# Attention into two gated layers on one core: the first tile's products in plain float32, its weights split only for the later tiles, conversion by whole blocks, and another order at layer two's border

## The chip, the cores and the metric

The kernel runs on one core of a Trainium2 chip. The metric is the device time in microseconds (us) of one execution; of several executions the median counts. The engines are TensorE (PE in the profile, with its weight loads as PEld), VectorE (DVE), ScalarE (ACT), GpSimd (POOL) and SyncE (SP), which here only issues DMAs.

## The reference

```python
# attention: q, k, v are [4, 8, 576, 64]; causal softmax plus a memory term
scores = np.where(causal, -1e9, q @ k.T / 8);  a = softmax(scores);  local = a @ v
mem_out = (phi(q) @ M_prev) / (phi(q) @ z_prev + 1e-6)     # phi(x) = elu(x) + 1
out = g * mem_out + (1 - g) * local                        # g = sigmoid(beta), one per head
x = out as [2304 tokens, 512]
# layer one and layer two: w_in [512, 2048], w_out [2048, 512] each
h = x @ w_in;  x = (h * sigmoid(1.702 * h)) @ w_out
h = x @ w_in;  x = (h * clip(h + 3, 0, 6) / 6) @ w_out
```

The weights arrive as float64, seen by the kernel as pairs of 32-bit words, and are made float32 on the chip.

## The kernel before

**Tiles.** The 2304 tokens are six tiles of 384. Tiles 0, 1, 3 and 4 hold the first 384 rows of a batch entry; tiles 2 and 5 hold the last 192 rows of two entries each. Attention runs by pairs of heads, four pairs to a segment (`scores`, `turn`, `mem_read`, `weigh`), and is emitted some pairs ahead of the layers: while tile t goes through layer one, attention makes the x of tile t + 1. `pump` sets the pace: `PG0` and `PG1` say over what share of a tile's 128 quarter-steps the attention steps are spread.

**Layers.** `moe` goes through units (layer, tile, f), f over 16 blocks of 128 hidden columns. A unit is four products into the bank h (`kk` 0 to 3, L302 to L304), a gate chain, and, `lag` units later, four products into the banks y0 to y3 (`emit_y`, L282 to L284). Each product is three matmuls on float32r operands that were split in two parts: w hi by x hi, w lo by x hi, w hi by x lo. In the first five tiles of layer one h has one bank and the lag is 1; from the last tile of layer one on h has three banks and the lag is 3.

**The gate.** ACT makes tanh (L254) or relu (L258) of h, DVE multiplies with h (L256, L260), ACT rounds to g hi (L263), and POOL, in tile 0 DVE, subtracts to get g lo (L265). x is split in the same way by `split_x` (ACT L247, DVE L248).

**Weight conversion.** `conv_w` takes a half block (w_in part a = 0 or w_out part a = 1 of one f; 128x512 pairs of words) through a chain in six stages: two DVE operations on the words (L197, L202); POOL adds a constant (L206) and ACT or DVE takes the absolute value (L208, L210); ACT takes the sign (L212); DVE makes the float32 value x in a temporary tile (L215); ACT rounds it to the hi part (L222); POOL (layer one) or DVE (layer two) subtracts for the lo part (L225). A chain is emitted stage by stage through `Chains.step`, once for every product; at most four halves are under way, since `conv_w` first finishes the half four before. The first operation is pinned in DVE's program order for layer one (`PIN`), free for layer two. The halves of layer one are converted during the attention of tile 0 and during tile 0's products; those of layer two from the last tile of layer one on, one every seven steps (`PR`).

**Order on the engines.** The instructions are put in each engine's queue by a planner with its own costs, within what `issue_after`, `after_gates` and `keep_in_program_order` fix.

**The border of the layers.** x of layer two's tile 0 is split after each of the last h products of layer one (`after_quarter`); layer two's first h products are emitted while three units of layer one's y are still pending.

Of the kernel before, what the change touches and what calls it, by code (L numbers as in the profile page):

```python
# [22 lines left out]
NT = 384  # L23
PRE = 4
KQ = 80
CR = 3.75
OFF = 3
PG0 = 0.55
# [25 lines left out]
AHEAD = 4  # L54
TF = 12
TWB = (1, 3)
EARLY = 3
P2 = 4
PR = 7
# [45 lines left out]
def attention_moe_kernel(ctx: ExitStack, tc: tile.TileContext, qk0, sk0, sk1, vm0, vm1, bb, w1, w2, out):  # L105
# [15 lines left out]

    wt = {}
    w_raw = {}
    w_gen = {}
    w_jobs = [(layer, f, a) for layer in range(2) for f in range(NF) for a in range(2)]
    w_at = [0, 0]
    w_temp = {}
# [22 lines left out]
    def load_w(n):  # L150


        while w_at[0] < min(n, len(w_jobs)):
            key = layer, f, a = w_jobs[w_at[0]]
            w_at[0] += 1
            if (layer, f, a) == (0, NF - 1, 0):
                for old in range(2 * TF, 2 * (TF + 1)):
                    gen = w_gen.get(w_jobs[old - 2])
                    if gen is not None:
                        chains.finish(gen)  # L160
                w_temp.clear()
            pool, tag = slot(*key)
            w_raw[key] = pool.tile([128, 2 * DM], I32, tag=tag, bufs=1, name=f"r{f}{a}")
            move(0, out=w_raw[key], in_=(w1, w2)[layer][f, a].bitcast(I32))

    def slot(layer, f, a):

        if layer == 1 and f < EARLY:
            return early[0], f"e{f}{a}"
        return wp, f"w{f - EARLY * layer}{a}"  # L170

    def temp(layer, f, a):

        if layer == 0 and f < TF:
            k = (2 * f + a) % 4
            if k // 2 not in w_temp:
                w_temp[k // 2] = wp.tile([128, 2, DM], F32, tag=f"w{NF - 1}{k // 2}", name="wtemp")
            return w_temp[k // 2][:, k % 2]
        pool, bufs = temps
        return pool.tile([128, DM], F32, tag="wt", bufs=bufs, name="wt")  # L180

    def conv_w():

        n = w_at[1]
        key = layer, f, a = w_jobs[n]
        if n >= 4 and w_jobs[n - 4] in w_gen:
            chains.finish(w_gen[w_jobs[n - 4]])
        w_at[1] += 1
        load_w(w_at[1])
        if layer == 0:  # L190
            load_w(min(2 * NF, w_at[1] + AHEAD))
        z = 2 if layer == 1 else int(2 * f + a >= 2 * PRE)
        words = w_raw.pop(key).rearrange("p (n two) -> p n two", two=2)
        lo, hi = words[:, :, 0], words[:, :, 1]

        def chain():
            first = DVE.tensor_scalar(  # L197
                out=lo, in0=lo, scalar1=29, scalar2=0x40000000, op0=ALU.logical_shift_right, op1=ALU.bitwise_or
            )
# [14 lines left out]
            x = temp(layer, f, a)  # L214
            DVE.scalar_tensor_tensor(  # L215
                out=x, in0=f32(lo), scalar=BIG, in1=f32(hi), op0=ALU.min, op1=ALU.mult
            )
            pool, tag = slot(layer, f, a)
            t = pool.tile([128, 2, DM], F32R, tag=tag, bufs=1, name=f"w{f}{a}")
            wt[key] = t  # L220
            yield
            ACT.copy(out=t[:, 0], in_=x)  # L222
            yield
            e = "DVE" if (2 * f + a) % WLE[z][1] < WLE[z][0] else "POOL"
            {"DVE": DVE, "POOL": POOL}[e].tensor_tensor(out=t[:, 1], in0=x, in1=f32(t[:, 0]), op=ALU.subtract)  # L225

        w_gen[key] = chains.start(after_gates(chain(), CB[layer]))

# [22 lines left out]
    def gate(layer, ti, h, g):  # L251
        t = gp.tile([128, NT], F32, tag="t", bufs=GB, name="t")
        if layer == 0:
            ACT.activation(out=t, in_=h, func=AF.Tanh, scale=0.851)  # L254
            yield
            d = DVE.scalar_tensor_tensor(out=t, in0=t, scalar=1.0, in1=h, op0=ALU.add, op1=ALU.mult)  # L256
# [8 lines left out]
        d = (DVE, POOL)[GLE[ti if layer == 0 else -1]].tensor_tensor(out=g[:, 1], in0=t, in1=f32(g[:, 0]), op=ALU.subtract)  # L265
        gated[("DVE", "POOL")[GLE[ti if layer == 0 else -1]]].append(d.ins)

    def moe(units, before_h, after_quarter, finish):
# [4 lines left out]
        def emit_y():  # L273
            layer, ti, f, g, gen = pend.pop(0)
            chains.finish(gen)
            w = need_w(layer, f, 1)
            if f == 0:
                for d in range(KD):
                    ys[d] = psy.tile([128, NT], F32, tag=f"y{d}", name=f"y{d}")
            for d in range(KD):  # L280
                o = d * 128
                PE.matmul(ys[d], lhsT=w[:, 0, o:o + 128], rhs=g[:, 0], start=(f == 0), stop=False)  # L282
                PE.matmul(ys[d], lhsT=w[:, 1, o:o + 128], rhs=g[:, 0], start=False, stop=False)  # L283
                PE.matmul(ys[d], lhsT=w[:, 0, o:o + 128], rhs=g[:, 1], start=False, stop=(f == NF - 1))  # L284
                if f == NF - 1:
                    finish(layer, ti, d, ys[d])
                chains.step()
                if d == KD - 1 and layer == 0 and ti == LAST:
                    load_w(2 * (NF + EARLY + f + 1))
                yield layer, ti, f  # L290

        ys = [None] * KD
        for layer, ti, f in units:
            before_h(layer, ti, f)
            w = need_w(layer, f, 0)
            h = phase["h"].tile([128, NT], F32, tag=phase["tag"], bufs=phase["bufs"], name="h")
# [12 lines left out]
            g = phase["g"].tile([128, 2, NT], F32R, tag="g", bufs=phase["lag"] + 1, name="g")  # L309
            gen = chains.start(gate(layer, ti, h, g))  # L310
# [87 lines left out]
    def attention(ap):  # L398
# [253 lines left out]
        def weigh(i):  # L652
# [28 lines left out]
            if ((0, ti), p) not in xr:  # L681
                xr[(0, ti), p] = xp.tile([128, NT], F32, tag=f"x{p}", name=f"x{p}")
# [55 lines left out]
    with ExitStack():  # L738
# [19 lines left out]
        POOL.memset(step_down, -STEP)  # L758

# [50 lines left out]
        stream = moe(units, before_h, after_quarter, finish)  # L810

        with tc.tile_pool(name="ap", bufs=2) as ap:
# [3 lines left out]
            for k, mark in enumerate(att):  # L816
# [3 lines left out]
                convert_to(min(2 * PRE, int(2 * PRE * k / KQ) + K0))  # L820
            convert_to(2 * PRE)
            banks[0] = 3
            phase["behind"] = lambda: marks[-1 - SLACK] if len(marks) > SLACK else None
            for kk in range(KD):
                split_x((0, 0), kk)
            qi, ti = 0, 0
            for layer, t, f in stream:
# [7 lines left out]
                if ti == 0:  # L835
                    convert_to(min(2 * NF, 2 * PRE + int(qi / CR)))
                pump((qi - OFF) / (PG0 * 128 / 36 if TILES[ti + 1][0][1] == 0 else PG1 * 128 / 57))

        with tc.tile_pool(name="x2p", bufs=2) as x2p:
# [4 lines left out]
            load_w(2 * (NF + EARLY))  # L844
# [64 lines left out]
```

## Time and profile before

| | before |
|---|---|
| median of 3 runs | 1082.98 us (1082.46 to 1084.0) |
| the profiled execution | 1084.36 us, span 1082.5 us |
| mean granted clock | 0.980 |
| PE busy | 1033.4 us, 95% of the span |
| DVE, ACT, POOL busy | 510.2, 498.8, 399.1 us |
| DMA | 71.91 MB, 19.7% of the span of 16 engines |

The busy shares are means over stages with different limits, so they are read by stages: tile 0 of layer one (50 to 188 us), a middle tile, the border of the layers (602 to 737 us), and layer two after it. The duration of a matmul in a row is its time from start to modelled end; matmuls overlap, so what one costs is the distance between starts.

### The profile page before, as it was taken

Reading aid. Unit: us, or ns where it says so; the run is one execution under the profiler, and the core shown is the slowest. Engines: PE = TensorE matmul, PEld = TensorE weight load, DVE = VectorE, ACT = ScalarE, POOL = GpSimd, SP = SyncE. Lnnn points to the kernel's source line nnn. Section 1 sums busy time; section 2 is a strip of 40 time slices with the busy share of each in tenths; the row PEclk is TensorE's granted clock in tenths of the full one; section 3 lists DMA queues with packets and bytes.
Section 4 is the critical chain, followed back from the end, with each engine's and each line's share of the span. In section 5 each row is a group of like instructions: output and inputs, shape, how many; then the busy total and the mean of one; then the engine's idle time right before and its main releaser. Section 6 shows DMA issues by size and latency. Waiting matters only on the chain. (4 is left out here: it accounts for less than half of the span.)

```text
span 1082.5 us, 16719 instructions
## 1 busy us (share of the span) xinstructions
PE 1033.4 (95%) x6153; PEld 940.3 (87%) x6153; DVE 510.2 (47%) x1372; ACT 498.8 (46%) x1152; POOL 399.1 (37%) x444
## 2 busy tenths in 40 slices
PE   7877888999999999999999997998999999999998
PEld 4566766888888888888889997998999999999998
DVE  6999997344544443333444598873121121211210
ACT  6757655334454454433333566764233232332322
POOL 4778765223333333222322454543222222222221
PEclk9888998999999999999999998999999999999999
DMA  6643321211121110211110684001010010100000
GB/s 227 239 158 103 127 69 36 68 45 59 28 76 37 38 55 25 59 30 60 30 30 16 246 324 140 30 1 59 1 31 30 1 59 1 31 30 1 30 1 29
DMA packets 29280, 71.91 MB, mean 66 GB/s; under 512 B 3600, under 2 KB 12816, under 8 KB 29200
## 3 DMA queue, kind: packets, MB, share of 16 engines
q1 hardware_dynamic: 29200, 70.86, 19.7%
q8 instruction: 48, 0.79, 0.3%
q14 instruction: 32, 0.26, 0.1%
HBM read 61.41 MB, written 9.44 MB: 65 GB/s over the span
## 5 line engine op out<-in xcount | busy, mean ns | idle before, releaser
L265 POOL TENSOR_TENSOR g<-t,g 128x384 fp32r<-128x384 f32 x176 | 185.1, 1052 | 473.1 <-ACT g L263 448.5
L302 PE MATMUL h<-xs,w 128*128 128x384 f32 x768 | 267.1, 348 | 16.1 <-DVE t L256 8.1
L282 PE MATMUL y<-g,w 128*128 128x384 f32 x768 | 260.4, 340 | 3.4 <-ACT g L263 3.3
L303 PE MATMUL h<-xs,w 128*128 128x384 f32 x768 | 260.1, 339 | 0.3 <-DVE w L225 0.3
L304 PE MATMUL h<-xs,w 128*128 128x384 f32 x768 | 260.3, 339 | 0.0
L283 PE MATMUL y<-g,w 128*128 128x384 f32 x768 | 259.2, 337 | 0.0
L284 PE MATMUL y<-g,w 128*128 128x384 f32 x768 | 244.1, 339 | 0.6 <-POOL g L265 0.6
L260 DVE SCALAR_TENSOR_TENSOR t<-t,h 128x384 f32<-128x384 f32 x96 | 53.1, 553 | 273.2 <-ACT t L258 273.2
L302 PEld LDWEIGHTS h<-xs,w 128*128 128x128 f32 x768 | 146.3, 191 | 24.7 <-DVE t L256 12.6
L282 PEld LDWEIGHTS y<-g,w 128*128 128x128 f32 x768 | 145.1, 189 | 7.0 <-ACT g L263 4.6
L284 PEld LDWEIGHTS y<-g,w 128*128 128x128 f32 x768 | 142.3, 188 | 6.7 <-issue 4.1
L303 PEld LDWEIGHTS h<-xs,w 128*128 128x128 f32 x768 | 146.6, 191 | 1.4 <-issue 0.8
L304 PEld LDWEIGHTS h<-xs,w 128*128 128x128 f32 x768 | 146.0, 190 | 1.1 <-issue 0.5
L283 PEld LDWEIGHTS y<-g,w 128*128 128x128 f32 x768 | 145.1, 189 | 1.4 <-issue 1.3
L263 ACT CAST g<-t 128x384 fp32r<-128x384 f32 x192 | 98.4, 513 | 95.1 <-DVE t L260 49.2
L258 ACT ACTIVATE t<-h,three 128x384 f32<-128x384 f32 x96 | 55.7, 580 | 170.5 <-PE h L304 170.5
L454 POOL TENSOR_SCALAR p<-p,st,omg 128x128 f32<-128x128 f32 (+3 forms) x128 | 91.8, 729 | 99.3 <-DVE st L450 44.7
L446 ACT ACTIVATE p<-s,st 128x256 f32<-128x256 f32 (+4 forms) x160 | 82.4, 521 | 69.6 <-DVE st L441 57.5
L441 DVE CUSTOM_DVE_ANT_0 s<-s,mask 128x128 f32<-128x128 f32 (+3 forms) x144 | 72.6, 526 | 85.0 <-PE s L381 84.1
L256 DVE SCALAR_TENSOR_TENSOR t<-t,h 128x384 f32<-128x384 f32 x96 | 52.7, 550 | 74.5 <-ACT t L254 70.3
L381 PE MATMUL s<-qk 64*128 64x256 f32 (+5 forms) x384 | 72.3, 466 | 12.2 <-issue 3.5
L254 ACT ACTIVATE t<-h 128x384 f32<-128x384 f32 x96 | 46.7, 490 | 67.9 <-PE h L304 65.1
(79 smaller groups left out, 1103.5 us busy)
## 6 DMA issues: line engine op xcount, KB each, us to landing
r<-in_w_dram SPq DMA_DIRECT2D x64, 512.0 KB, 6.2
vm<-in_vm_dram SPq DMA_DIRECT2D x16, 386.0 KB, 3.0
qk<-in_qk_dram SPq DMA_DIRECT2D x16, 384.0 KB, 3.5
qk<-in_sk_dram SPq DMA_DIRECT2D x32, 192.0 KB, 3.3
x2d<-yo SPq DMA_DIRECT2D x24, 192.0 KB, 1.9
xr<-x2d SPq DMA_DIRECT2D x24, 192.0 KB, 3.1
out_dram<-yo SPq DMA_DIRECT2D x24, 192.0 KB, 1.9
vm<-in_vm_dram SPq DMA_DIRECT2D x16, 258.0 KB, 2.7
```

What stands on the lines that cost most here:

```text
L263: gated["ACT"].append(ACT.copy(out=g[:, 0], in_=t).ins)
L265: d = (DVE, POOL)[GLE[ti if layer == 0 else -1]].tensor_tensor(out=g[:, 1], in0=t, in1=f32(g[:, 0]), op=ALU.subtract)
L282: PE.matmul(ys[d], lhsT=w[:, 0, o:o + 128], rhs=g[:, 0], start=(f == 0), stop=False)
L283: PE.matmul(ys[d], lhsT=w[:, 1, o:o + 128], rhs=g[:, 0], start=False, stop=False)
L284: PE.matmul(ys[d], lhsT=w[:, 0, o:o + 128], rhs=g[:, 1], start=False, stop=(f == NF - 1))
L302: PE.matmul(h, lhsT=w[:, 0, c:c + 128], rhs=x[:, 0], start=(kk == 0), stop=False)
L303: PE.matmul(h, lhsT=w[:, 1, c:c + 128], rhs=x[:, 0], start=False, stop=False)
L304: PE.matmul(h, lhsT=w[:, 0, c:c + 128], rhs=x[:, 1], start=False, stop=(kk == KD - 1))
L381: ins = PE.matmul(out, **args).ins
L441: DVE.tensor_tensor_reduce(out=o, in0=o, in1=m, scale=-SCALE, scalar=init, op0=ALU.add, op1=ALU.min, accum_out=out)
L446: return ACT.activation(out=dst, in_=o, func=AF.Exp, scale=-1.0, bias=m, accum_out=s)
L454: (DVE, POOL)[e[norms[0] % len(e)]].tensor_scalar(out=dst, in0=dst, scalar1=s, scalar2=w, op0=ALU.mult, op1=ALU.mult)
```

## The change

It keeps what is computed and changes these parts.

1. Tile 0 of layer one uses plain float32 operands: one matmul call per product on the unsplit weight, x and g. There the split of x, the rounding of g and the subtraction for g lo are left out (`exact`).
2. `conv_w` takes a whole block f (both parts a, 128x1024) at a time. For layer one the chain ends with the float32 value, written in the raw block's own place (`wx[f]`). One block before must be fully emitted. For layer two the constant is added on ACT instead of POOL, and the split is part of the chain.
3. Layer one's weights are split for tiles 1 to 5 by `part_w`: from step 104 of tile 0 on, one block every 8 steps, two DMAs copy the block's value to temporary tiles, then two ACT roundings and two DVE subtractions write the parts where the block was.
4. At the border `between` splits x for layer two, then all pending y of layer one is emitted, then layer two's first h.
5. The last three units of layer one subtract for g lo on DVE (`GLL`); paces are restated: `CR`, `PG0` (0.85 in tile 0, 0.55 as before otherwise), `PR` 14 for whole blocks, `AHEAD`, `W0`, `TWB`.

```diff
-CR = 3.75
+CR = 7.5
-PG0 = 0.55
+PG0 = (0.85, 0.55)
+GLL = 3
-W0 = (2, 3)
-WLE = ((0, 2), (0, 2), (2, 2))
-ABS = ((0, 2), (1, 2), (2, 2))
+W0 = (1, 2)
+ABS = ((0, 1), (1, 2), (1, 1))
-AHEAD = 4
-TF = 12
-TWB = (1, 3)
+AHEAD = 2
+TWB = (3, 2)
+S2 = 104
+SR = 8
-PR = 7
+PR = 14
...
     def conv_w():
-        n = w_at[1]
-        key = layer, f, a = w_jobs[n]
-        if n >= 4 and w_jobs[n - 4] in w_gen:
-            chains.finish(w_gen[w_jobs[n - 4]])
+        key = layer, f = w_jobs[w_at[1]]
+        if (layer, f - 1) in w_gen:
+            chains.finish(w_gen[layer, f - 1])
...
+        words = raw.rearrange("p a (n two) -> p a n two", two=2)
+        lo, hi = words[:, :, :, 0], words[:, :, :, 1]
+        if layer == 0:
+            wx[f] = f32(raw)[:, :, 0:DM]
...
-            POOL.tensor_scalar(out=f32(hi), in0=f32(hi), scalar1=STEP, scalar2=1.0, op0=ALU.add, op1=ALU.mult)
+            if layer == 0:
+                POOL.tensor_scalar(out=f32(hi), in0=f32(hi), scalar1=STEP, scalar2=1.0, op0=ALU.add, op1=ALU.mult)
+            else:
+                ACT.activation(out=f32(hi), in_=f32(hi), func=AF.Identity, bias=step_up[:, 0:1])
...
+            x = [wx[f]] if layer == 0 else [temp() for _ in range(2)]
+            for k, to in enumerate(x):
+                at = slice(None) if layer == 0 else k
+                DVE.scalar_tensor_tensor(
+                    out=to, in0=f32(lo)[:, at], scalar=BIG, in1=f32(hi)[:, at], op0=ALU.min, op1=ALU.mult
+                )
+            if layer == 1:
+                yield
+                yield from parts(layer, f, x)
...
+    def parts(layer, f, x):
+        pool, tag = slot(layer, f)
+        t = pool.tile([128, 2, 2, DM], F32R, tag=tag, bufs=1, name=f"w{f}")
+        wt[layer, f] = t
+        for a in range(2):
+            ACT.copy(out=t[:, 0, a], in_=x[a])
+        yield
+        for a in range(2):
+            DVE.tensor_tensor(out=t[:, 1, a], in0=x[a], in1=f32(t[:, 0, a]), op=ALU.subtract)
+
+    def part_w(f):
+        def chain():
+            x = [temp() for _ in range(2)]
+            for a in range(2):
+                move(4, out=x[a], in_=wx[f][:, a])
+            del wx[f]
+            yield
+            yield from parts(0, f, x)
+        if (0, f - 1) in w_gen:
+            chains.finish(w_gen[0, f - 1])
+        w_gen[0, f] = chains.start(after_gates(chain(), CB[1]))
...
+        exact = (layer, ti) == (0, 0)
+        to = g[:, 0] if exact else t
...
+        if exact:
+            return
...
+                if (layer, ti) == (0, 0):
+                    PE.matmul(ys[d], lhsT=w[:, o:o + 128], rhs=g[:, 0], start=(f == 0), stop=(f == NF - 1))
...
+            if (layer, ti, f) == (1, 0, 0):
+                between()
+                while pend:
+                    yield from emit_y()
...
+                    if exact:
+                        PE.matmul(h, lhsT=w[:, c:c + 128], rhs=x, start=first, stop=last)
...
-            if layer == 0 and f == NF - 1:
-                split_x((0, ti + 1) if ti < LAST else (1, 0), kk)
+            if layer == 0 and f == NF - 1 and ti < LAST:
+                split_x((0, ti + 1), kk)
...
+        def between():
+            for kk in range(KD):
+                split_x((1, 0), kk)
...
-            for kk in range(KD):
-                split_x((0, 0), kk)
...
-                    convert_to(min(2 * NF, 2 * PRE + int(qi / CR)))
+                    convert_to(min(NF, PRE + int(qi / CR)))
+                if ti < 2 and 128 * ti + qi >= S2:
+                    part_to(1 + (128 * ti + qi - S2) // SR)
```

## Rows read from the trace of the kernel before

**Rows 1.** Busy time of each engine, granted clock and DMA share in four stages.
```profile
50.00:188.00 138.00, 115.54 (x636) 94.42 (x635) 128.57 (x288) 86.52 (x192) 97.41 (x87) 0.90 0.32 108
188.00:278.00 90.00, 89.64 (x582) 78.44 (x581) 37.42 (x145) 36.38 (x99) 26.86 (x33) 1.00 0.18 53
602.00:737.00 135.00, 127.11 (x709) 123.75 (x707) 111.43 (x162) 93.35 (x169) 66.30 (x62) 0.97 0.40 145
800.00:1082.00 282.00, 279.14 (x1611) 278.82 (x1609) 44.73 (x82) 88.83 (x168) 66.79 (x66) 1.00 0.07 23
```
**Rows 2.** DVE's groups by line in 50 to 188 us: busy, mean ns, idle before.
```profile
L202 DVE SCALAR_TENSOR_TENSOR r<-r 128x512 int32<-128x512 int32 x29 | 26.1, 909 | 0.1
L197 DVE TENSOR_SCALAR r<-r 128x512 int32<-128x512 int32 x29 | 19.8, 684 | 0.1
L215 DVE SCALAR_TENSOR_TENSOR wtemp<-r 128x512 f32<-128x512 f32 x21 | 18.3, 871 | 0.8 <-ACT r L212 0.8
...
L265 DVE TENSOR_TENSOR g<-t,g 128x384 fp32r<-128x384 f32 x16 | 11.6, 728 | 0.0
```
**Rows 3.** Single lines over the whole span: shortest, median and longest duration in ns.
```profile
L197 DVE TENSOR_SCALAR r<-r x64: 410/421/1517, 22.0 to 730.8; 128x512 int32<-128x512 int32 x64
L202 DVE SCALAR_TENSOR_TENSOR r<-r x64: 673/747/1778, 22.4 to 731.8; 128x512 int32<-128x512 int32 x64
L215 DVE SCALAR_TENSOR_TENSOR wtemp<-r x24: 667/681/1770, 25.8 to 145.4; 128x512 f32<-128x512 f32 x24
```
**Rows 4.** POOL's groups by line in 50 to 188 us.
```profile
L225 POOL TENSOR_TENSOR w<-wtemp,w 128x512 fp32r<-128x512 f32 x22 | 32.3, 1474 | 9.8 <-ACT w L222 9.8
L206 POOL TENSOR_SCALAR r<-r 128x512 f32<-128x512 f32 x29 | 25.0, 867 | 13.1 <-DVE r L202 10.5 <-DMA qk<-in_sk_dram 1.2 <-DVE st L449 0.7
L225 POOL TENSOR_TENSOR w<-wt,w 128x512 fp32r<-128x512 f32 x8 | 10.9, 1364 | 6.9 <-ACT w L222 6.9
```
**Rows 5.** Timeline of PE in layer two, 24 matmuls apart: start and duration in us.
```profile
800.26 0.33 PE L282 MATMUL y<-g,w 128*128 128x384 f32 x1
...
804.42 0.33 PE L282 MATMUL y<-g,w 128*128 128x384 f32 x1
```
**Rows 6.** Timeline of PE at plain float32 matmuls of the attention.
```profile
24.50 0.83 PE L366 MATMUL mem<-vm,phi 128*128 128x130 f32 x6
25.18 0.49 PE L396 MATMUL t<-ident,p 128*128 128x128 f32 x3
```
**Rows 7.** One DVE operation at two widths, groups by shape over the span.
```profile
L441 DVE CUSTOM_DVE_ANT_0 s<-s,mask 128x512 f32<-128x512 f32 x48 | 32.9, 704 | 51.1 <-PE s L381 51.1
...
L441 DVE CUSTOM_DVE_ANT_0 s<-s,mask 128x128 f32<-128x128 f32 x32 | 9.7, 308 | 7.2 <-PE s L381 7.2
```
**Rows 8.** Busy times in the two disturbed stretches of the border.
```profile
650.00:670.00 20.00, 14.15 (x65) 12.41 (x64) 17.02 (x26) 14.32 (x27) 8.74 (x8) 0.83 0.37 127
730.00:750.00 20.00, 17.03 (x86) 15.82 (x85) 9.69 (x16) 9.99 (x20) 6.92 (x7) 0.91 0.13 40
```
**Rows 9.** PE's longest wait in 600 to 760 us: total, times, longest in us.
```profile
PE h L302 <- ACT xs L247: 5.1, 2, 3.7
```
**Rows 10.** Conversion groups of ACT and DVE in 602 to 737 us.
```profile
L212 ACT ACTIVATE r<-r,step_down 128x512 f32<-128x512 f32 x32 | 24.2, 768 | 6.2 <-POOL r L206 6.0
L208 ACT ACTIVATE r<-r 128x512 f32<-128x512 f32 x32 | 21.7, 681 | 23.2 <-DVE r L202 23.1
L222 ACT CAST w<-wt 128x512 fp32r<-128x512 f32 x32 | 19.6, 619 | 7.9 <-DVE wt L215 7.6
L263 ACT CAST g<-t 128x384 fp32r<-128x384 f32 x30 | 15.3, 510 | 1.6 <-DVE t L256 1.3 <-DVE t L260 0.2
...
L202 DVE SCALAR_TENSOR_TENSOR r<-r 128x512 int32<-128x512 int32 x32 | 38.2, 1209 | 0.1
L225 DVE TENSOR_TENSOR w<-wt,w 128x512 fp32r<-128x512 f32 x32 | 25.3, 798 | 2.7 <-ACT w L222 2.7
```
**Rows 11.** DMA issues over the span: count, KB each, median us to landing.
```profile
xr<-x2d SPq DMA_DIRECT2D x24, 192.0 KB, 3.1
```

More of the change, by code (lines that the diff above doesn't have):

```diff
@@ L124, in attention_moe_kernel @@
     w_gen = {}
-    w_jobs = [(layer, f, a) for layer in range(2) for f in range(NF) for a in range(2)]
+    w_jobs = [(layer, f) for layer in range(2) for f in range(NF)]
     w_at = [0, 0]
-    w_temp = {}
+    w_parted = [0]
     temps = []
@@ L153, in load_w, with slot @@
         while w_at[0] < min(n, len(w_jobs)):
[L154 removed]
+            key = layer, f = w_jobs[w_at[0]]
             w_at[0] += 1
[L156 to L166, printed above, removed]
[L168 to L180 removed]
+            pool, tag = slot(layer, f)
+            w_raw[key] = pool.tile([128, 2, 2 * DM], I32, tag=tag, bufs=1, name=f"r{f}")
+            for a in range(2):
+                move(0, out=w_raw[key][:, a], in_=(w1, w2)[layer][f, a].bitcast(I32))
+    def slot(layer, f):
+        if layer == 1 and f < EARLY:
+            return early[0], f"e{f}"
+        return wp, f"w{f - EARLY * layer}"
     def conv_w():
[L184 to L187 removed]
+        key = layer, f = w_jobs[w_at[1]]
+        if (layer, f - 1) in w_gen:
+            chains.finish(w_gen[layer, f - 1])
         w_at[1] += 1
@@ L213, in chain, with temp @@
             yield
[L214 to L220, printed above, removed]
-            yield
[L222 to L227, printed above, removed]
+            x = [wx[f]] if layer == 0 else [temp() for _ in range(2)]
[7 more added lines that the diff above has]
+                yield from parts(layer, f, x)
+        w_gen[key] = chains.start(after_gates(chain(), CB[layer]))
+    def temp():
+        pool, bufs = temps
+        return pool.tile([128, DM], F32, tag="wt", bufs=bufs, name="wt")
+    def parts(layer, f, x):
+        pool, tag = slot(layer, f)
+        t = pool.tile([128, 2, 2, DM], F32R, tag=tag, bufs=1, name=f"w{f}")
[8 more added lines that the diff above has]
+            x = [temp() for _ in range(2)]
+            for a in range(2):
+                move(4, out=x[a], in_=wx[f][:, a])
+            del wx[f]
+            yield
+            yield from parts(0, f, x)
+        if (0, f - 1) in w_gen:
+            chains.finish(w_gen[0, f - 1])
+        w_gen[0, f] = chains.start(after_gates(chain(), CB[1]))
     def convert_to(n):
@@ L231, in convert_to, with part_to, need_w @@
             conv_w()
-    def need_w(layer, f, a):
-        convert_to(2 * (NF * layer + f) + a + 1)
-        gen = w_gen.pop((layer, f, a), None)
+    def part_to(n):
+        while w_parted[0] < min(n, NF):
+            w_parted[0] += 1
+            part_w(w_parted[0] - 1)
+    def need_w(layer, ti, f, a):
+        convert_to(NF * layer + f + 1)
+        if (layer, ti) != (0, 0) and layer == 0:
+            part_to(f + 1)
+        gen = w_gen.pop((layer, f), None)
         if gen is not None:
             chains.finish(gen)
-        return wt[layer, f, a]
+        return wx[f][:, a] if (layer, ti) == (0, 0) else wt[layer, f][:, :, a]
     xr = {}
@@ L255, in gate @@
             yield
-            d = DVE.scalar_tensor_tensor(out=t, in0=t, scalar=1.0, in1=h, op0=ALU.add, op1=ALU.mult)
+            d = DVE.scalar_tensor_tensor(out=to, in0=t, scalar=1.0, in1=h, op0=ALU.add, op1=ALU.mult)
         else:
@@ L264, in gate, with moe @@
         yield
-        d = (DVE, POOL)[GLE[ti if layer == 0 else -1]].tensor_tensor(out=g[:, 1], in0=t, in1=f32(g[:, 0]), op=ALU.subtract)
-        gated[("DVE", "POOL")[GLE[ti if layer == 0 else -1]]].append(d.ins)
-    def moe(units, before_h, after_quarter, finish):
+        e = "POOL" if GLE[ti if layer == 0 else -1] and not (layer == 0 and ti == LAST and f >= NF - GLL) else "DVE"
+        d = {"DVE": DVE, "POOL": POOL}[e].tensor_tensor(out=g[:, 1], in0=t, in1=f32(g[:, 0]), op=ALU.subtract)
+        gated[e].append(d.ins)
+    def moe(units, before_h, after_quarter, between, finish):
         pend = []
@@ L275, in emit_y @@
             chains.finish(gen)
-            w = need_w(layer, f, 1)
+            w = need_w(layer, ti, f, 1)
             if f == 0:
@@ L308, in moe @@
                     yield layer, ti, f
-            g = phase["g"].tile([128, 2, NT], F32R, tag="g", bufs=phase["lag"] + 1, name="g")
-            gen = chains.start(gate(layer, ti, h, g))
+            g = phase["g"].tile([128, 2, NT], F32 if exact else F32R, tag="g", bufs=phase["lag"] + 1, name="g")
+            gen = chains.start(gate(layer, ti, f, h, g))
             chains.step()
@@ L758, in attention_moe_kernel @@
         POOL.memset(step_down, -STEP)
+        step_up = const.tile([128, 1], F32, name="step_up")
+        POOL.memset(step_up, STEP)
         gall = const.tile([128, 4, H], F32, name="gall")
```

50 lines of the change are left out of this document (29 added, 21 removed).

## The prediction

> **What bounds the kernel now.** I read the busy times by stages first. From 800 us on PE is full, at full clock: 279 of 282 us, and a matmul of a split product starts every 0.173 us (24 of them in 4.16 us) [rows 1, 5]. A middle tile is the same, 89.6 of 90 us. Whatever leaves such a stretch on another engine is worth nothing there. Two stretches are different. In tile 0 of layer one (50 to 188 us) DVE is busy 128.6 of 138 us, and PE's granted clock is 0.90 on average [rows 1]. So tile 0 is set by DVE. There the reader is to look at DVE's groups: the three large ones of the weight conversion (L202, L197, L215) take 909, 684 and 871 ns on average where their shortest take 673, 410 and 667 [rows 2, 3]. The longest take over 1500. Meanwhile POOL is busy 97.4 us of the 138 [rows 1], 43.2 of them with the weights' lo parts [rows 4]. These three read and write SBUF alone, and seem to be held while POOL works. The other weak stretch is the border of the layers, 602 to 737 us: PE is busy 127.1 of 135. In 650 to 670 us it starts 65 matmuls where 20 / 0.173 = 115 fit, a loss of 50 x 0.173 = 8.7 us; in 730 to 750 us 86, a loss of 5.1 [rows 8]. The longest wait there is for the split of x, 3.7 us [rows 9].
>
> **Tile 0: what goes from DVE.** The conversion has 29 halves left in the window. The three groups come to 26.1 + 19.8 + 29 x 0.871 = 71.2 us (eight of the L215 write another tile; I charge them the same mean) [rows 2]. At the shortest durations they would be 29 x (0.673 + 0.410 + 0.667) = 50.8; so 20.4 us are stretch.
> - Whole blocks: one DVE operation at 128 and 512 columns takes 308 and 704 ns, so 176 ns do not depend on width [rows 7]. Three operations less per block, 14.5 blocks: 7.7 us saved. The abs operations, fewer too, I leave at nothing.
> - The weights' lo parts leave POOL: 43.2 us of 97.4 [rows 4, 1]. If stretch follows POOL's busy time, 44% of 20.4 goes: 9.0 us. Bounds: nothing (if the stretch is the remaining POOL work's) and 20.4. I take 9.0, since both kinds of POOL work are of similar length.
> - g lo leaves DVE: 11.6 us [rows 2].
> - Split of the first blocks comes back from step 104 on: three blocks, two subtractions each at 0.798 (the same operation at the border [rows 10]): 4.8 us.
>
> DVE's new load is 128.6 - 7.7 - 9.0 - 11.6 + 4.8 = 105.1 us. That is all for a tile that took 138.
>
> **Tile 0: what PE gets.** Here the change costs. Before, a product is three matmuls, 3 x 0.173 = 0.520 us. No row shows a plain float32 product of 384 columns with 128x128 weights. The nearest are the attention's plain matmuls of 130 columns: a pair of a first segment makes three such calls and has six matmuls in the trace, so a call is two; six take 25.18 - 24.50 = 0.68 us, 0.113 each [rows 6]. Scaled to 384 columns a matmul is 0.335, a product 0.669. From below: two matmuls no faster than split ones, 0.347. From above: the scaled value, as a fixed part would only lower it. I take 0.669, because the row is plain float32 too. So 128 products cost 85.6 us instead of 66.6: 19.0 more. The remaining 636 - 384 = 252 matmuls of the window are attention's; at 0.113 they are 28.5 us [rows 1, 6] (that window may hold a few products of the tile before or after). PE's load becomes 114.1 us and passes DVE's 105.1. PE becomes the bound.
>
> The Trainium skill speaks against the change at this place: the page "FP8 and Floating Point Precision", section "TensorE Precision Notes", says that true FP32 takes four passes through the array. With a split product as three single passes that would be 4/3 of 0.520, or 0.693 a product, 3.1 us more for the tile than my scaled row. No row of this trace has the product itself.
>
> How well is a bound filled? DVE filled 128.6 of 138, 0.93 [rows 1]. With two engines nearly level I take the same: 114.1 / 0.93 = 122.7 us. **Tile 0 falls from 138 to 122.7, 15.3 us less.** Bounds: 114 (PE as full as in a middle tile) to 138.
>
> ACT loses in the same window the rounding of weights and of g; it was busy 86.5 of 138, so nothing follows. The split of x ahead of tile 0 is hidden behind attention's last matmuls and I cost its removal at nothing; if that cover were gone it would be about 1 us (a rounding of 0.51 as L263 and a subtraction like L265).
>
> **Tile 1: what comes back.** Thirteen blocks are split here. DVE gets 26 subtractions at 0.798, 20.7 us, on its 37.4 of 90; ACT gets 26 roundings at 0.619, 16.1 us, on 36.4 [rows 1, 10]. Both stay under 60 of 90, so PE keeps the bound. But h has one bank: the next h waits for tanh and multiply (about 0.51, as L263, and 0.57, by rows 7: 0.176 + 384 x 0.00103), hidden behind the y products of 4 x 0.520 = 2.08. An operation just begun delays these by at most 0.62 on ACT and 0.80 on DVE; 1.08 + 1.42 = 2.50, beyond the cover by 0.42. Over thirteen units that is at most 5.5 us, and a second operation in a row would add. Below it is nothing. I take 3.
>
> The copies are 32 DMAs of 256 KB on SP's queue. A 192 KB transfer lands in 3.1 us [rows 11], 256 KB then in about 4.1, and DMA is busy 0.18 of the tile [rows 1]. Each waits for a temporary tile (three, and a block takes two), that is, for the subtractions of the block before; behind it in SP's queue stand attention's loads, and the stores of tile 0's y, whose three buffers the gate shares. Loads are prefetched two pairs ahead. A late store would hold the gate on ACT; the copies begin 24 steps, about 20 us, before their block is used. So I take nothing, and up to 4 us above.
>
> **The border.** Splitting x ahead of the pending y gives it three y blocks of cover, 3 x 2.08 = 6.2 us, where the trace shows a wait of 3.7 and then cold PE. That cover is longer than the wait. Of the 8.7 us lost in 650 to 670 I take 6.0 as recovered; the gate waits before the split stay. Bounds 0 and 8.7. The loss of 5.1 in 730 to 750 I leave as it is; it can go, or grow (below). POOL loses the 32 constant additions (about 0.9 each) and ACT gets them at about 0.68, as L208 [rows 10]: 21.8 us on 93.4 of 135 [rows 1], so ACT reaches 115, or 0.85. It still fits.
>
> **Sum** against the profiled execution's 1084.4 us: 1084.4 - 15.3 + 3 - 6 = 1066.1. That execution is 1.4 above the median of the runs; on the median's scale 1064.7, stated as 1064.
>
> **Rivals.**
> *The conversion chain in series.* One block must be emitted before the next starts, and layer one's first operation is pinned behind it on DVE, where four halves could overlap before. At the window's means a block is DVE 1.19 + 1.64, POOL 1.73, ACT 1.54 (L212), DVE 1.57: 7.7 us; at DVE's shortest 6.2. With tile 0 at 122.7, block 15 is wanted 115 us after its start; with two blocks ready by then, 14 remain, 8.2 us each. From there on it decides. If queues add 1.5 to 7.7, 14 x 9.2 = 129, plus the last unit's 7, is 136: tile 0 gains 2 and the time is 1064.7 + 13.3 = 1078. For: DVE is a full queue. Against: it becomes emptier by 23 us, POOL by 43.
>
> *The border's conversion too slow: the other side.* Layer two's block, in whole pieces, is DVE 2 x 0.42 (L197's median) + 2 x 1.21, ACT three passes 2 x (0.68 + 0.68 + 0.77), then 2 x 0.68 on DVE (L215's median), 2 x 0.62 on ACT, 2 x 0.80 on DVE [rows 3, 10]: 11.7 us in a row, 10.7 with two fixed parts of 0.18 saved and the first rounding beside the second L215. Before, 32 halves took the stretch of 135 us, 8.4 a block, with four halves under way. If blocks go one by one at 10.7, the last is ready 16 x 2.3 = 37 us later, and layer two's tile 0 waits: 1065 + 37 = 1102. It decides from 8.4 + 18.3 / 16 = 9.5 us a block on. For it: two temporary tiles, just one block's. Against it: the first operations aren't pinned there, so the next block can start on DVE while ACT works; ACT's own work is 2 x 2.75 a block at most, and 2 x 0.51 per 4.16 us for gates, 7.3 us a block at the limit.
>
> *PE not relieved at all.* If tile 0's clock falls as before (0.90), a plain product costs up to twice as much in those stretches, 114.1 / 0.90 = 126.8 before any wait, and with 0.93 136. Then the conversion gain is spent on PE: 1064.7 + 13 = 1078, the first rival's time.
>
> **From this to the numbers.** A measurement of this kernel tells about 0.2%, 2.2 us. Forecast (1050 to 1073): 0.55. First and third rival (1073 to 1080.8): 0.20. No change: 0.06. Slower, by the border: 0.14. Better than 1050, with tile 0 at PE's load and both border losses gone (1084.4 - 24 - 13.8 = 1047): 0.05. Faster is 0.80. The range 1046 to 1082 takes in the bounds and all but the slow side; the forecast's own is 1050 to 1073.
>
> **What would show it.** Right: tile 0 ends near 173 us, its plain matmuls start 0.33 us apart, DVE's L202 means less per column and POOL is busy near 54 us there; tile 1 stays 90 to 93; PE's wait for the split of x at the border is gone. Wrong: in tile 0 PE waits for L215's successor (first rival), a clock below 0.9 (third), or PE waits at the border for ACT's rounding or DVE's subtraction, with the last conversion later than 737 (second).

## The result, and the profile after

| | before | after |
|---|---|---|
| median | 1082.72 us (1082.27 to 1084.0) | 1063.97 us (1063.95 to 1064.1) |
| ratio, 95% interval | | 0.9825 [0.9808, 0.9842] |
| span, mean clock | 1082.5 us, 0.980 | 1062.2 us, 0.990 |
| PE, DVE, ACT, POOL busy | 1033.4, 510.2, 498.8, 399.1 us | 1035.6, 486.7, 495.0, 317.9 us |

The kernel is 1.75% faster, 18.8 us. To see where, I cut every trace at the same marks: PE's first matmul for h, and ACT's first reading of y (yo) of each tile. The lengths in us, with those of the experiments (each experiment's ratio below is against the kernel before on its own chip):

| run | median | first h | tile 0 | tile 1 | tiles 2 to 4 | border (tile 5 and layer two's tile 0) |
|---|---|---|---|---|---|---|
| before | 1082.7 | 50.2 | 142.1 | 108.2 | 306.7 | 143.9 |
| after | 1064.0 | 45.9 | 123.5 | 117.3 | 307.3 | 136.8 |
| e1_border_undone | 1057.4 | 46.1 | 123.5 | 117.3 | 307.3 | 130.2 |
| e2_border_only | 1084.3 | 50.4 | 140.6 | 108.1 | 306.7 | 145.3 |
| e3_pace_055 | 1068.3 | 46.9 | 130.1 | 114.6 | 307.0 | 136.2 |
| e8_own_yo | 1060.0 | 48.9 | 122.6 | 117.2 | 307.4 | 130.8 |
| e4_no_lo | 1056.4 | 47.9 | 111.2 | 114.1 | 306.7 | 142.9 |
| e5_one_matmul | 1077.2 | 49.0 | 138.1 | 106.7 | 306.7 | 142.9 |
| e7_no_lo_parts | 1065.3 | 45.6 | 125.1 | 117.5 | 306.9 | 136.2 |
| e6_pool_add | 1068.9 | 47.0 | 123.7 | 117.3 | 307.4 | 139.9 |
| e9_lo_on_dve | 1074.0 | 47.7 | 130.3 | 112.5 | 306.7 | 143.1 |
| e10_act_add | 1071.8 | 50.8 | 140.6 | 108.3 | 306.7 | 132.1 |
| e11_all_act | 1053.5 | 48.1 | 118.3 | 117.3 | 307.0 | 130.6 |
| e12_pool_out | 1054.1 | 47.0 | 126.6 | 107.4 | 306.7 | 131.7 |

Layer two after its tile 0 takes 331.4 to 331.8 us in all of them. So the change starts tile 0 4.3 us earlier, takes 18.6 us from tile 0, gives 9.1 back in tile 1, and takes 7.1 at the border.

The busy times of the changed kernel by stages (stretch, length, PE, PEld, DVE, ACT, POOL, granted clock, DMA), to be read beside [rows 1]:
```profile
46.00:166.00 120.00, 112.44 (x461) 64.87 (x463) 95.94 (x200) 59.20 (x117) 48.80 (x40) 0.99 0.41 144
166.00:276.00 110.00, 108.27 (x705) 91.48 (x702) 70.63 (x222) 59.19 (x154) 33.35 (x43) 1.00 0.35 114
592.00:727.00 135.00, 129.50 (x730) 128.86 (x729) 103.44 (x141) 106.59 (x161) 39.64 (x30) 0.97 0.39 140
```
In tile 0 the fuller engine is no longer DVE (128.6 of 138) but PE (112.4 of 120), and the clock goes from 0.90 to 0.99. Cut at 90 us, the tile has two parts:
```profile
46.00:90.00 44.00, 36.94 (x153) 21.00 (x154) 40.96 (x83) 23.67 (x48) 27.67 (x21) 0.96 0.75 266
90.00:166.00 76.00, 75.50 (x310) 43.87 (x310) 54.98 (x118) 35.52 (x70) 21.13 (x20) 1.00 0.21 73
```
In the first DVE is still the full engine (41.0 of 44, PE 36.9); in the second it is PE (75.5 of 76). DVE's and POOL's conversion groups there, whole blocks now, answer to [rows 2, 4] (the changed kernel has other line numbers: DVE's L187, L192 and L210 are L197, L202 and L215 of the kernel before, POOL's L197 is its L206, ACT's L205 its L212):
```profile
L192 DVE SCALAR_TENSOR_TENSOR r<-r 128x1024 int32<-128x1024 int32 x15 | 21.5, 1433 | 0.2
L210 DVE SCALAR_TENSOR_TENSOR r<-r 128x1024 f32<-128x1024 f32 x15 | 18.6, 1240 | 8.8 <-ACT r L205 8.8
L187 DVE TENSOR_SCALAR r<-r 128x1024 int32<-128x1024 int32 x15 | 11.4, 757 | 0.0
```
```profile
L197 POOL TENSOR_SCALAR r<-r 128x1024 f32<-128x1024 f32 x15 | 19.1, 1276 | 31.3 <-DVE r L192 21.3 <-DVE st L496 8.8 <-DMA r<-in_w_dram 1.2
```
A block costs DVE 1.433 + 1.240 + 0.757 = 3.43 us against 2 x (0.909 + 0.684 + 0.871) = 4.93 before. The plain products on PE's timeline, to set beside [rows 5, 6]:
```profile
91.78 2.74 PE L317 MATMUL y<-g,r 128*128 128x384 f32 x8
94.36 0.49 PE L443 MATMUL t<-ident,p 128*128 128x128 f32 x3
```
Eight matmuls take 94.36 - 91.78 = 2.58 us, 0.3225 each. A plain call shows as two matmuls in the trace, so a plain product is 0.645 us against 0.520 split. At the border the split of x no longer holds PE, but something else does (waits of PE from 580 to 760 us; then the disturbed stretch and the one that was the second, cf. [rows 8, 9]):
```profile
PE h L348 <- DVE t L291: 4.8, 1, 4.8
PE h L348 <- DVE t L287: 0.7, 1, 0.7
```
```profile
650.00:670.00 20.00, 15.24 (x72) 14.92 (x71) 14.43 (x21) 14.99 (x25) 2.56 (x3) 0.83 0.27 93
710.00:730.00 20.00, 20.00 (x117) 20.00 (x116) 8.22 (x15) 11.08 (x20) 6.26 (x6) 1.00 0.13 40
```
The first stretch is hardly better (72 matmuls for 65). The second, where the last weights came just in time, is clean: 117 for 86.

### The profile page after: what moved, and what is told of

Read it like the earlier page. It is cut to its first block, busy times and chain, and to the rows that moved or that the text cites. A ratio compares the mean times of both kernels' runs of the same rounds, so it can differ in the third digit from the quotient of the medians.

```text
span 1062.2 us, 16317 instructions
## 1 busy us (share of the span) xinstructions
PE 1035.6 (97%) x6025; PEld 916.2 (86%) x6025; DVE 486.7 (46%) x1297; ACT 495.0 (47%) x1094; POOL 317.9 (30%) x362
## 4 chain that ended last, share of the span: by engine, by line
PE 84%; DVE 6%; ACT 5%; DMA 2%; issue 2%; POOL 1%; SPq 0%; ACTq 0%; DVEq 0%; POOLq 0%
PE h L348 11%; PE y L319 11%; PE y L321 11%; PE y L320 10%; PE h L351 10%; PE h L350 10%; PE o L428 5%; PE s L428 5%; PE y L317 3%; PE t L443 3%; PE h L346 3%; PE mem L413 1%; DVE r L192 1%; ACT p L493 1%; DVE s L488 1%
## 5 line engine op out<-in xcount | busy, mean ns | idle before, releaser
L348 PE MATMUL h<-xs,w 128*128 128x384 f32 x704 | 242.9, 345 | 6.0 <-DVE t L291 4.8
L319 PE MATMUL y<-g,w 128*128 128x384 f32 x704 | 237.3, 337 | 0.5 <-ACT g L296 0.5
L351 PE MATMUL h<-xs,w 128*128 128x384 f32 x704 | 237.1, 337 | 0.0
L350 PE MATMUL h<-xs,w 128*128 128x384 f32 x704 | 236.8, 336 | 0.0
L320 PE MATMUL y<-g,w 128*128 128x384 f32 x704 | 236.2, 336 | 0.0
L321 PE MATMUL y<-g,w 128*128 128x384 f32 x704 | 224.4, 337 | 0.0
L291 DVE SCALAR_TENSOR_TENSOR t<-t,h 128x384 f32<-128x384 f32 x96 | 53.0, 553 | 274.1 <-ACT t L289 273.9
L348 PEld LDWEIGHTS h<-xs,w 128*128 128x128 f32 x704 | 133.2, 189 | 13.9 <-issue 5.8
L321 PEld LDWEIGHTS y<-g,w 128*128 128x128 f32 x704 | 130.4, 188 | 5.5 <-issue 4.9
L319 PEld LDWEIGHTS y<-g,w 128*128 128x128 f32 x704 | 132.2, 188 | 2.9 <-issue 1.0
L351 PEld LDWEIGHTS h<-xs,w 128*128 128x128 f32 x704 | 133.0, 189 | 0.5 <-issue 0.5
L350 PEld LDWEIGHTS h<-xs,w 128*128 128x128 f32 x704 | 133.3, 189 | 0.0
L320 PEld LDWEIGHTS y<-g,w 128*128 128x128 f32 x704 | 132.2, 188 | 0.5 <-issue 0.5
L296 ACT CAST g<-t 128x384 fp32r<-128x384 f32 x176 | 90.2, 514 | 89.5 <-DVE t L291 48.3
L493 ACT ACTIVATE p<-s,st 128x512 f32<-128x512 f32 (+4 forms) x160 | 82.4, 521 | 80.3 <-DVE st L488 66.7
L285 ACT ACTIVATE t<-h 128x384 f32<-128x384 f32 x96 | 46.9, 491 | 60.6 <-PE h L351 53.2
L287 DVE SCALAR_TENSOR_TENSOR t<-t,h 128x384 f32<-128x384 f32 x80 | 44.1, 552 | 64.9 <-ACT t L285 56.4
```

Source lines behind the costliest of these rows:

```text
L348: PE.matmul(h, lhsT=w[:, 0, c:c + 128], rhs=x[:, 0], start=first, stop=False)
L493: return ACT.activation(out=dst, in_=o, func=AF.Exp, scale=-1.0, bias=m, accum_out=s)
```

## The experiments

**The border's order, alone and taken back.** In e1 the changed kernel loses `between`; in e2 the kernel before gets it.
```diff
# e1: changed kernel          (e2: the same lines added to the kernel before)
-            if (layer, ti, f) == (1, 0, 0):
-                between()
-                while pend:
-                    yield from emit_y()
-            if layer == 0 and f == NF - 1 and ti < LAST:
-                split_x((0, ti + 1), kk)
+            if layer == 0 and f == NF - 1:
+                split_x((0, ti + 1) if ti < LAST else (1, 0), kk)
```


> The changed kernel with the border's order as before: x of layer two's tile 0 is split after each of the last h products of layer one, and layer two's h starts while three units of y are pending. If the order gave the 7 us that the border gained (the stores of tile 5 to tile 6 in the two traces), the time rises from 1064 to 1069 to 1072, and PE waits for the split of x again. Rival, that whole blocks with the constant on ACT gave it: the time stays below 1066.

> The kernel before with the border's new order alone. If the order is worth 6 us by itself: 1075 to 1078, from 1083. Rival, that it pays only with the faster conversion, since before the last weights of layer two came just in time at 731 to 737 us: the gain of the first stretch is lost again in the second and the time stays within 2 us of 1083.

Measured: e1 1057.4 us, 0.976 [0.9745, 0.9774] of before, 6.6 us faster than the changed kernel; e2 1084.3, 1.0007 [0.9996, 1.0017]. The time in e1 is below 1066, as the rival had it; that the order costs 6.6 us neither answer had. In e2 it gains nothing. Without the new order PE stays full through the border, here from 590 to 660 and 660 to 730 us in e1:
```profile
590.00:660.00 70.00, 69.26 (x400) 68.94 (x399) 56.98 (x79) 59.06 (x90) 18.65 (x15) 1.00 0.72 260
660.00:730.00 70.00, 69.72 (x399) 68.60 (x398) 48.47 (x65) 52.05 (x83) 21.23 (x18) 1.00 0.10 35
```
In e2 the wait for the split near 660 us is gone, but PE now waits in the same stretch for g of the pending units (waits from 590 to 760 us; then 650 to 680 and 730 to 750 us, e2 first and the kernel before second):
```profile
PE y L284 <- POOL g L265: 3.6, 3, 2.8
PE y L282 <- ACT g L263: 3.6, 2, 2.0
```
```profile
650.00:680.00 30.00, 22.72 (x102) 20.28 (x101) 22.99 (x36) 20.87 (x40) 14.21 (x12) 0.83 0.39 133
730.00:750.00 20.00, 18.44 (x96) 17.78 (x95) 9.23 (x15) 9.68 (x19) 6.81 (x7) 0.91 0.13 40
```
```profile
650.00:680.00 30.00, 24.15 (x123) 22.41 (x122) 24.70 (x38) 20.09 (x37) 13.97 (x13) 0.89 0.36 119
730.00:750.00 20.00, 17.03 (x86) 15.82 (x85) 9.69 (x16) 9.99 (x20) 6.92 (x7) 0.91 0.13 40
```
PE starts 102 matmuls for 123 in the first stretch, and 96 for 86 in the second. So the time stays, as the rival said, but the other way round: the loss is in the first stretch and not at the last weights. The changed kernel makes the g lo of these three units on DVE (`GLL`), which e2 leaves out, so e2 is the new order without that help. What `GLL` is worth was not tested by itself.

**What the new order waits for.** In the changed kernel all of tile 5's y is finished before layer two's first gate. ACT's timeline there:
```profile
656.77 1.27 ACT L371 ACTIVATE yo<-y 128x384 f32<-128x384 f32 x3
657.88 1.23 ACT L205 ACTIVATE r<-r,step_down 128x1024 f32<-128x1024 f32 x1
658.97 1.27 ACT L199 ACTIVATE r<-r,step_up 128x1024 f32<-128x1024 f32 x1
660.08 1.14 ACT L201 ACTIVATE r<-r 128x1024 f32<-128x1024 f32 x1
661.07 0.52 ACT L371 ACTIVATE yo<-y 128x384 f32<-128x384 f32 x1
661.44 1.10 ACT L289 ACTIVATE t<-h,three 128x384 f32<-128x384 f32 x2
```
Three yo take the three tiles t, which the gate uses too; the fourth comes 4.3 us and the first relu 4.7 us after the first, behind three conversion passes. With three h banks full, PE stands still, 4.8 us in the row above. e8 gives the four yo other tiles:
```diff
+        if layer == 0 and ti == LAST:
+            t = xp.tile([128, NT], F32, tag=f"x{d}", name="yo")
```


> The changed kernel with the last four results of layer one (yo of tile 5) in the tiles that x of layer one has left, not in the three tiles t that the gate uses too. In the changed trace PE waits 4.8 us at the border for DVE's multiply, which waits for relu on ACT, which starts only after the fourth yo. If the shared tiles make that wait, it goes with the cold stretch behind it: 1056 to 1059. Rival, that the conversion's operations in ACT's queue hold relu: 1062 to 1064.

Measured 1060.0, 0.978 [0.9765, 0.9794], between my two ranges. What is left of PE's wait from 580 to 760 us:
```profile
PE h L348 <- DVE t L291: 1.5, 1, 1.5
```
The wait falls from 4.8 to 1.5 us and the border from 136.8 to 130.8, so the shared tiles made most of it. The time is above the lower range, and first h comes 3 us later here, although PE, DVE, ACT and POOL run the same instructions in the same order up to there; from 20 to 30 us the granted clock is 0.73 in this trace and 1.00 in the changed kernel's.

**What made the border faster, then.** e6 is e1 with layer two's constant back on POOL; e10 is the kernel before with that constant on ACT, halves and order kept.
```diff
# e6 on e1; e10 on the kernel before moves the same operation the other way
-            if layer == 0:
+            if layer >= 0:
                 POOL.tensor_scalar(out=f32(hi), in0=f32(hi), scalar1=STEP, ...)
```


> The changed kernel with the border's order as before (1057.4 measured) and layer two's constant back on POOL, whole blocks kept. If whole blocks alone made the border faster: 1056 to 1059. If the constant's move to ACT made it, by taking POOL's passes off DVE's operands and off the chain: 1062 to 1068, with L192 longer than the 1.2 us it takes there now.

> The kernel before with layer two's constant on ACT instead of POOL, by halves as before, the border's order as before. Put back on POOL in whole blocks it cost 11.5 us. If the engine of the constant alone decides: 1070 to 1075 from 1083. Rival, that whole blocks are needed with it, since ACT pays a fixed part for each of two passes a half: 1079 or more.

Measured: e6 1068.9, 11.5 us slower than e1; e10 1071.8, 0.9904 [0.989, 0.9919] of before. The engine of the constant decides; whole blocks are not needed for this gain. In e6 the border is still 4.0 us shorter than before the change (139.9 for 143.9); which of the other parts gives that was not separated. DVE's groups from 590 to 730 us, e1 first and e6 second:
```profile
L210 DVE SCALAR_TENSOR_TENSOR wt<-r 128x512 f32<-128x512 f32 x32 | 25.1, 815 | 9.1 <-ACT r L205 9.1
L192 DVE SCALAR_TENSOR_TENSOR r<-r 128x1024 int32<-128x1024 int32 x16 | 22.0, 1377 | 0.2
```
```profile
L210 DVE SCALAR_TENSOR_TENSOR wt<-r 128x512 f32<-128x512 f32 x32 | 31.1, 1005 | 8.6 <-ACT r L205 8.6
L192 DVE SCALAR_TENSOR_TENSOR r<-r 128x1024 int32<-128x1024 int32 x16 | 26.2, 1638 | 0.2
```
DVE runs the same instructions in both, and these two groups take a fifth longer when POOL has the constant. Whether that stretch or a slower chain through POOL costs more was not separated. In e10 the busy times from 602 to 737 us, beside the third of [rows 1]:
```profile
602.00:737.00 135.00, 132.67 (x758) 131.05 (x757) 110.42 (x170) 114.29 (x212) 42.56 (x34) 1.00 0.42 148
```
ACT rises from 93 to 114 us of 135 and PE starts 758 matmuls for 709.

**Tile 0: who set it, and what POOL does to DVE.** e5 takes away PE's work in the kernel before, e4 POOL's.
```diff
# e5, in tile 0 of layer one: one matmul of three
+                if not one:
                     PE.matmul(ys[d], lhsT=w[:, 1, o:o + 128], rhs=g[:, 0], ...)
                     PE.matmul(ys[d], lhsT=w[:, 0, o:o + 128], rhs=g[:, 1], ...)
# e4, layer one: no subtraction for the lo part
+            if layer == 0:
+                return
             yield
             e = "DVE" if (2 * f + a) % WLE[z][1] < WLE[z][0] else "POOL"
```


> The kernel before with one of the three matmuls of each product in tile 0 of layer one (the two that correct with lo parts are left out there); all conversion stays. PE's load in tile 0 falls by 2 x 128 x 0.173 = 44 us. If DVE set tile 0 before the change, the time falls by at most 5 us from 1083, and may rise where the emptier PE gets a lower clock. Rival, that PE with its clock set it: a fall of 15 us or more.

> The kernel before with POOL's subtraction for the lo part of layer one's weights left out (43.2 us in tile 0); PE reads the hi part in its place, so its load stays. If POOL's work stretches DVE's conversion: L202, L197 and L215 fall from 909, 684 and 871 ns towards 800, 560 and 780 in tile 0, DVE gets 9 us back there, and the time falls by 8 to 12 us from 1083. Rival, that the stretch has another cause: the means stay and the time stays within 3 us.

Measured: e5 1077.2, 0.9944 [0.9929, 0.9959], 6 us of the 44 taken away, a little over the 5 I allowed; from 50 to 183 us the granted clock is 0.72 and DVE 126.9 of 133 busy:
```profile
50.00:183.00 133.00, 87.95 (x385) 57.66 (x385) 126.90 (x282) 85.30 (x188) 94.27 (x87) 0.72 0.32 109
```
DVE set tile 0. e4 is 1056.4, 0.9754 [0.974, 0.9769]: 27 us, more than the whole change, where I had put 8 to 12. DVE's groups and the busy times of e4 from 50 to 160 us:
```profile
L202 DVE SCALAR_TENSOR_TENSOR r<-r 128x512 int32<-128x512 int32 x28 | 20.2, 723 | 0.1
L215 DVE SCALAR_TENSOR_TENSOR wtemp<-r 128x512 f32<-128x512 f32 x21 | 14.9, 712 | 2.4 <-ACT r L212 2.4
L197 DVE TENSOR_SCALAR r<-r 128x512 int32<-128x512 int32 x27 | 13.1, 485 | 1.5 <-DMA r<-in_w_dram 1.5
```
```profile
50.00:160.00 110.00, 101.17 (x611) 85.57 (x610) 100.23 (x270) 83.66 (x187) 50.51 (x55) 1.00 0.37 123
```
Of the excess over the shortest durations, 0.236 + 0.274 + 0.204 = 0.71 us a half [rows 2, 3], 0.050 + 0.075 + 0.045 = 0.17 is left, although POOL is still busy half of the time. So this one operation of POOL made three quarters of the stretch, and PE's clock rose to 1.00 with its removal. The three groups give back 29 x (0.71 - 0.17) = 15.7 us; other groups of DVE got shorter too (the subtraction for g lo from 728 to 626 ns), but the whole of the 27 us was not traced. The trace of the kernel before shows it instruction by instruction; here POOL, then DVE beside it:
```profile
74.31 2.71 POOL L225 TENSOR_TENSOR w<-wtemp,w 128x512 fp32r<-128x512 f32 x2
79.62 2.93 POOL L454 TENSOR_SCALAR p<-p,st,omg 128x384 f32<-128x384 f32 x2
```
```profile
74.49 1.37 DVE L197 TENSOR_SCALAR r<-r 128x512 int32<-128x512 int32 x1
75.90 1.67 DVE L202 SCALAR_TENSOR_TENSOR r<-r 128x512 int32<-128x512 int32 x1
81.17 0.42 DVE L197 TENSOR_SCALAR r<-r 128x512 int32<-128x512 int32 x1
81.50 0.68 DVE L202 SCALAR_TENSOR_TENSOR r<-r 128x512 int32<-128x512 int32 x1
```
Beside the subtraction (L225) the two operations take 1.37 and 1.67 us, beside attention's work on POOL (L454) 0.42 and 0.68, about their shortest. Of all 86 instructions of L197, L202 and L215 from 50 to 188 us, the 31 that overlap the subtraction are 17.7 us over their shortest durations in sum, the 34 that overlap other POOL work 2.3, and the 21 that overlap none 0.2.

**The same without leaving anything out.** e9 puts the subtraction on DVE in the kernel before; e11 is e1 with layer one's constant on ACT too; e12 is the kernel before with both, that is, with POOL out of all conversion and nothing else of the change.
```diff
# e9 and e12
-WLE = ((0, 2), (0, 2), (2, 2))
+WLE = ((2, 2), (2, 2), (2, 2))
# e12 (e11 the same in the changed kernel)
-            POOL.tensor_scalar(out=f32(hi), in0=f32(hi), scalar1=STEP, scalar2=1.0, op0=ALU.add, op1=ALU.mult)
+            ACT.activation(out=f32(hi), in_=f32(hi), func=AF.Identity, bias=step_up[:, 0:1])
```


> The kernel before with layer one's lo subtractions on DVE instead of POOL; all products stay split. Left out altogether they gave 27 us and a tile 0 of 111 us, with DVE busy 100 of 110 in 50 to 160 us. On DVE they cost 29 x 0.70 = 20 us there: about 120 us of DVE work, at a fill of 0.93 a tile 0 of 129, so 1070 to 1074. If that holds, taking the subtraction off POOL alone is worth a good half of the change, and plain float32 with the late split the rest. Rival, that DVE loses in its own subtractions what it gains in stretch: 1081 to 1085.

> The changed kernel with the border's order as before (1057.4 measured) and layer one's constant on ACT too, so that POOL has no conversion work at all. If PE with its plain products sets tile 0 now (112 us busy of 120): 1054 to 1058. Rival, that DVE's remaining stretch and POOL's queue still set its first 40 us: 1047 to 1053. Third outcome, ACT's longer queue delays tanh: 1059 or more.

> The kernel before with POOL out of all conversion: layer one's lo subtractions on DVE and the constant on ACT in both layers. Halves, split products in every tile and the border's order stay. The two moves gave 8.5 and 10.3 us alone, in different stretches, and layer one's constant off POOL gave 4 in the changed kernel: added up, 1083 - 23 = 1060. If that holds, all that plain float32, whole blocks and the late split buy over it is the 1053.5 of the kernel with all constants on ACT: 6 to 7 us. Rival, that ACT in tile 0 becomes the bound with two more passes a block beside its roundings (about 85 + 22 of 128 us): 1063 or more.

Measured: e9 1074.0, 0.9928 [0.9912, 0.9945], in the expected range, 7.9 us and so less than half of the change's 18.8; L202 takes 708 ns there from 50 to 178 us, so its fall in e4 is not owed to the work left out. e11 is 1053.5, 0.9735 [0.9721, 0.975], between the range for "PE sets tile 0" and that for DVE's stretch in its first 40 us; e12 1054.1, 0.9744 [0.9728, 0.976], 6 us better than my sum of the two moves. e11 and e12 cannot be told apart. The busy times of tile 0, e11 first (46 to 166 us), then e12 (50 to 170):
```profile
46.00:166.00 120.00, 115.55 (x488) 67.81 (x489) 94.30 (x214) 80.34 (x146) 25.86 (x27) 1.00 0.45 155
```
```profile
50.00:170.00 120.00, 105.54 (x620) 87.61 (x621) 113.42 (x303) 99.74 (x213) 28.79 (x27) 0.96 0.36 113
```
In e11 tile 0 is 5.2 us shorter than in e1 (118.3 for 123.5) with the same products, and first h comes 2.0 later; so PE alone did not set tile 0 in the changed kernel. Now PE is the full engine in e11 and DVE in e12, and tiles 0 and 1 together take 235.6 and 234.0 us. Plain float32, whole blocks and the late split buy nothing that this shows over POOL's absence.

**Tile 1.** e3 sets the pace back, e7 leaves DVE's late subtractions out.
```diff
# e3
-PG0 = (0.85, 0.55)
+PG0 = (0.55, 0.55)
# e7, in parts()
+        if layer == 0:
+            return
         yield
         for a in range(2):
             DVE.tensor_tensor(out=t[:, 1, a], ...)
```


> The changed kernel with attention's pace in tile 0 at 0.55 as before, not 0.85. In the changed kernel tile 1 has 367 attention matmuls instead of 316 and lasts 9 us longer. If that is work moved by the pace, tile 1 falls by about 6 us here, tile 0 rises by as much, and the total stays at 1062 to 1066. Rival, that the slower pace is what keeps DVE free in tile 0: 1070 or more. Second rival, that the 9 us of tile 1 are the weight splits there: tile 1 keeps its length.

> The changed kernel with DVE's subtractions for layer one's lo parts left out (32 of about 0.7 us, 26 of them in tile 1); PE reads the hi part instead. 51 more attention matmuls lie in tile 1 than before, at about 0.13 us each 6.6 of its 9.1 longer, so the splits can have cost 2.5. If they did through DVE, tile 1 falls by 1 to 3 us and the time to 1061 to 1063. Rival, that ACT's roundings or the copies cost it: within 0.7 us of 1064. Second rival, that DVE's load is what makes tile 1 long: a fall of 5 us or more.

Measured: e3 1068.3, between my answers: tile 1 falls by 2.7 only (354 attention matmuls, not 316), tile 0 rises by 6.6, so the slower pace is worth 4 us. Of the 51 moved matmuls 13 are the pace's. The other 38 came with the rest of the change, and they do not follow from a shorter tile 0: the changed kernel, e1 and e11 all have 217 in tile 0 and 367 in tile 1, whether tile 0 takes 123.5 or 118.3 us, and e12 has 264 in 126.6. e7 is 1065.3, outside all three answers, though its interval takes in the changed kernel's ratio: leaving out DVE's subtractions gains nothing. PE is idle 1.9 of tile 1's 117.3 us, for 0.9 of 108.2 before, so waiting can have added 1.0 us; the rest of the 2.5 stays open.

## Why the prediction was right, and where not

The time, 1064 (the sum gave 1064.7), came out to 0.1 us, and that is luck. Forecast and measured were 0 and -4.3 us for the start, -15.3 and -18.6 for tile 0, +3 and +9.1 for tile 1, 0 and +0.6 for tiles 2 to 4, and -6.0 and -7.1 for the border, where two errors of opposite sign hide in one number.

- **Tile 0, the bound and its price: right in the main.** DVE set it (e5); of the changed tile DVE still fills the first 44 us and PE the rest, at 112.4 of 120 in all, where I had 114.1 / 0.93 = 122.7; DVE has 95.9 where I had 105.1. About 6.6 of the 18.6 us only moved to tile 1 (below): the two tiles together lost 9.5, where I had 12.3. The plain product is 0.645 us, 3.6% under the scaled row. The page "FP8 and Floating Point Precision" of the Trainium skill, section "TensorE Precision Notes", gives true FP32 four passes; at the length of a split matmul each, my estimate from it, a product would take 0.693. Here it is 1.24 split products, not 4/3, and the measurement decides.
- **The stretch: right in kind, mis-sized.** I gave POOL's subtraction 9.0 of the 20.4 us, in proportion to its busy time. e4 shows three quarters, 15.7 us. I took both kinds of POOL work to be of similar length; [rows 4] have 1474 ns against 867. If the changed kernel got the same back, that is 6.7 of the 9.2 us by which DVE came out emptier than forecast. The page "GPSIMD Engine Reference" of the Trainium skill, section "1. Specifications", says that POOL shares its SBUF interfaces with VectorE and contends with VectorE's instructions in a two-port mode or with two SBUF inputs. The runs agree for two inputs: L202 falls from 909 to 723 ns in e4 and the multiply with h, which reads one operand from PSUM, takes 0.54 us in both. L197 has one input and falls too, from 684 to 485; in which mode it runs no trace here shows.
- **Start: I had nothing, it was 4.3 us.** What made it is not shown: with the same instructions up to there, first h came at 45.9 us in the changed kernel and at 48.9 in e8, with another granted clock.
- **Tile 1: +3 forecast, +9.1 measured.** 51 attention matmuls came over from tile 0, at about 0.13 us (29.8 us for 237 in [rows 1]'s second stretch, of which 345 are products) 6.6 us. The remaining 2.5 us are near my 3, but not by the waits that I had reckoned with: e7 shows nothing for DVE's subtractions, and PE's idle time grew by 1.0.
- **The border: the step that failed.** I wrote that splitting x ahead of the pending y would recover 6.0 us, and that the constant's move from POOL to ACT merely fits. The border did gain 7.1, and for the opposite reasons: the order costs 6.6 us (e1), for the most part since the gate and four yo share three tiles (e8), and the constant's move, put at nothing, is worth 11.5 (e6). I had the row for it, L202 at 1209 ns at the border with 673 as its shortest [rows 10, 3], and didn't apply to it what I had argued for tile 0.
- **Rivals.** The chain in series shows as 8.8 us of DVE waiting for L205 in tile 0, 6.8 of them after 90 us, where PE is full. The slow conversion at the border did not come: its last block is done before 727 us. PE's clock in tile 0 stayed at 0.99.

## What to carry to other kernels

When an engine is full, compare each group's mean with its shortest before looking for less work: here DVE's nearly full 138 us held 20 us of stretch, nearly all of it beside POOL's work, and moving POOL's share of the conversion to busier engines (e12) gave 28 us with four lines. A saving argued in one stage should be looked for in every stage that runs the same instructions. A part of a change that looks free should be run without: the border's order cost as much as a third of the gain, and the changed kernel without it (1057.4, and 1053.5 with all constants on ACT too) beats both kernels.

## What was not expected of the hardware

POOL's subtraction of two SBUF operands, 1.47 us long, stretched DVE's operations far more than POOL's other work in the same tile: with 50.5 of 110 us of POOL left, DVE's L202 took 723 ns where its shortest is 673. What in POOL's operation decides this (two inputs, length, the moment at which it starts) was not separated. One input does not keep it from holding DVE: at the border of e6, L210 takes 684 ns beside no POOL instruction and 1.2 us on average beside the constant alone, and the constant costs L192 0.26 us a block. And a plain float32 product of 384 columns cost 0.645 us, 1.24 times the three matmuls of a split one, so the extra PE load of a whole tile was only 16 us.
